# Loading Q and K weights in pieces of three, six and seven heads, and storing half-pass V rows in another row order, in a two-layer recurrent-attention and GLU kernel

## The chip, the cores and the metric

The kernel runs on one core of a Trainium2 chip. The metric is the device time of one execution in microseconds, given as a median of several runs; lower is better. The profile is one execution recorded by the hardware profiler, and its times are microseconds from the start of its span unless marked ns. PE is TensorE (PEld its weight loads), ACT ScalarE, DVE VectorE, POOL GpSimd and SP SyncE; SP and POOL issue the DMAs here.

## The reference

Two blocks alternate twice with the same weights: A, attention that carries a memory of 8 rows from one segment of 32 tokens to the next, and B, a gated feed-forward layer. All data are bfloat16.

```python
# x (1,2048,512), mem0 (1,8,512), Wq/Wk/Wv (512,32,128), Wo (32,128,512)
# w_gate/w_up (512,1792), w_down (1792,512)
def A(x, mem0, Wq, Wk, Wv, Wo):
    mem, outs = mem0, []
    for s in range(64):                                    # one segment after another
        h = concat([mem, x[:, 32*s:32*(s+1)]], axis=1)     # 8 + 32 rows
        q, k, v = (einsum('btd,dhe->bhte', h, W) for W in (Wq, Wk, Wv))
        p = softmax(where(mask, q @ k.T * 128**-0.5, -1e9))
        o = einsum('bhte,hed->btd', p @ v, Wo)
        mem = o[:, :8]                                     # goes to the next segment
        outs.append(o[:, 8:])
    return concat(outs, axis=1)
def B(x): return (sigmoid(x @ w_gate) * (x @ w_up)) @ w_down
x = x + A(layernorm(x)); x = x + B(layernorm(x))
x = x + A(layernorm(x)); x = x + B(layernorm(x))
```

The mask (`(idx[:, None] < 8) | (idx[:, None] >= idx[None, :])` over the 40 rows) is causal for the segment's rows and open for the memory rows; it is the same for all segments.

## The kernel before

**Steps.** The 64 segments of a layer must go one after another, because each gives the next its memory rows. The kernel runs 70 steps; step t works on segment t of the first layer and on segment t-6 of the second together, 80 columns of activations (40 where only one layer has a segment). The heads go in pairs u and 16+u, three pairs to a group: heads 0 to 2 with 16 to 18, then 3 to 5 with 19 to 21, and so on, the last group being heads 15 and 31. A group's work is Q and K projections (L890), scores (L904), softmax on DVE and ACT, the transposition of the probabilities (L947), their product with V (L973) and the output projection (L991). Feed-forward blocks of 128 rows (L1093, L1117) and layer norms with their transposes (L662, L1061) are woven into the steps.

**V at the start.** The V rows of x don't depend on the memory, so those of the first blocks of the first layer are computed ahead, in passes of 128 rows by 512 columns (`v_pass`, matmuls L693). A piece of 64 rows that is left over goes through `v_half` (L730): its two halves of columns lie in partitions 0 to 63 and 64 to 127 of a bank, and of each 64 rows 32 belong to one octet of rows of four segments and 32 to two octets of two segments, put there by `take_part`. V rows of 32 rows go as strips (L815). A pass is evacuated by ACT or DVE casts (L1230, L1232) into one of nine boot buffers; these are the tiles of the feed-forward weight rings (wd, wg and wu, three each), which have no other use yet. From there DMAs on SP or POOL (L1226) store the rows in a DRAM scratch, scr, of which each step later loads its own into vsb. A boot buffer may be filled again once its store has landed.

**Weight loads.** `load_weights` adds all of them as SP tasks (L592): Wv in eight pieces of four heads (512 KB), and for each group of heads Wq, Wk and Wo in a piece for the heads u and one for the heads 16+u. A piece of three heads of Wq or Wk has rows of 768 bytes in DRAM, four per partition; a piece of one head has rows of 256 bytes.

**Order.** Nothing is issued as the code is written. Each operation is a task of a planner, with engines that may do it, a duration, a latency, the bytes moved and the buffers that it needs. A list scheduler (`forward`) gives each free engine the ready task of highest rank, and the ranks of all tasks are a string in the source, SEQUENCE, that `plan` decodes:

```python
for k, (q,) in enumerate(struct.iter_unpack("<H", code)):
    T[left.pop(q)].tail = -float(k)
```

The planner's estimates of when a DMA lands come from `lat` and `nb`. From the planned times `warm` also decides where filler matmuls on a constant tile, `hot` (L1216), go: before a planned gap of more than 250 ns on PE, up to some hundreds of ns each. Engines run their own instruction lists in order. SP's DMAs use eight semaphores in turn, so each SP DMA waits until the one eight before it has landed, and a store on SP that waits for its cast holds up the loads behind it.

The diff moves lines a little: those up to L600 stand one line higher in the changed kernel, those from L620 on two lines lower.

Of the kernel before, what the change touches and what calls it, by code (L numbers as in the profile page):

```python
# [53 lines left out]
;Aht@pIrb8fB#p5?Q#$k*OKvZZTq^c3OM%bV44b=*R*ZTyW=(F)eXpo=!dnjd%&eFWe?4v9B9J-6{(d-LCut;#!E)o@XKL;|1Yh}DX~>av(XnTcNY5yDmuUNDYpk)1hbP~Icf*@B%SY3<$N!PMdC+w  # L54
TzC*H?wh$B-*Ih~y~Z^1eU45ybkQ1*)!rl+2M7#!1kA=M>_00gM+A4yerPR?|M?Mj6^>>JOVW=CEf+cd3@>&Nfi0vId6NWR);FU?#N7i-E<e}?kQ5;smk7+$yR>6M$&vA+ka>GT!8=_b4-#fP#)eF7
^yFAVNqaBx;!Z*DxPH}w4u4hwLD|Xk-(55Lk^B_BDfkRj%d!v=C<*w7SG;+fg+&T)>)vE^_U=fY&kC>YwKQIya^N!=lH>FlpJ`Jr&lF|=A)fY+g;i{E@r#X;(VDk3V2MMXacuh+Y1k_asM6Wlyelal
#hat)UmCRL92k7baU(yGZ`~C!81W~7P5Erk>AYc<Vay?}YFcMj2ofpnp$(sP&YA3~nf~n+b1fFy?|Zym`QSa144a*IfxPvGj&Q1ek!IqLN$jiF41N6_7PG1D?N__fhI#wYegIrLSdO>RI&L#ADzYcB
9Qqa8r^xHgLyr2s6(Q^~qr%E_$NJ+TpJ_bc{R>AcDm>XZ4K<5#ddGdVwMU;&cRuZ|Sp~k`OZ$e|X_~sQ@384vzE1LEOy7FI`;?xf^#@MMQ)L6bC_!Zn4S4CHx9Vjn^H}pFj3R+|IJ2mzre;noNVd$S
`{%;vED%u54cw3M^F8VWNicF9{B~XUq?7A1595()pJ)9U7U(TRXvIYfie-lrSI2C)aZ1BBh3$_bQ;!I-B=8ScYh1ck&O!bB=K^(6{|r6Qx~A%7Guq$r@Iax)(DGfYMGmfWTtN`TiNx0^a_h-)zaQ;Y
Bg~_fxFI1YgW5VrkU}+v(OG0q+i!<|tAlPcRfvDusTf+wG<zAh-6L;+Y1?sI#2|g1{X&hwViH*}otG=?Uzck!7(XzcfK!b2s0y$`SNOr$pn;5(vR*N@6t6GIu9c&BiE<wNN?P(QqaXRd3M2ScK!LD`  # L60
7NE8fpYJ@UG|VxPeYSAG0la_&djDUlCG|bBoZOzAT#$(zHi(qOLpXAuXb5%<ke>jX1k1`o2(mU?ngq;3!G;hMQLm2&9MTEUYd^USvXFM#vQ$cKmjg>LrQvGCuN0;hmD;jcN{gk}oA#{rr~t7er6x;>
4TAPsm6b5FLH-g|Nf9h4giYb{D&c`|4)4`L+JTg9TM;~}=IotkUY(*Y!dPX~EqzNqLnvA&8*(y?XY|Ec+`KUE@_SSE)gkFi<&UF6JtvvpbP{*<I0G^z6$#&pA}^v95^Q4FK#<`jp&L`QSey9`{hytp
ep4|DPRnnzJfR5<$bbinu=f`jwczBNxe3uhZ<*z*5#J~4a?5s>6axJof)V}FxLuSWLQ`X$p%|GAo3ni>PtV+JzEAC$o%TiCe#d7B$K5bY%WL%|Y?`a4x@DA(YsP8dw{qC8hys!6@G=TJ3;?U)VFlx0
p<M<>KJllT(z)CRu8?`e3^R_R7%q?S32qi7rh98c7=(LFh!0=aD^hH1fNfXqg+Sja7$z4P_WGLKlHYlxk!E{x!eD5T8C@MZ?8P+s8nOs}&1S4ol`b-NnC>Xi=go6~%Yjg-4mHO!zq-ODIoX(~$HahI
@>xN0b)~I`DIDj5VKMa;CZ!v*mkbmOJ)#~W9x(W_v;<nswK`+PTq}ipg*!qKSltnE+$xw7Xt>R@wAQgZ(cg;enc1@7fR_`9(15bKuOa8wjwP|W7E?oWno808^?XT*fvZ96JauH_vO6Tmg0YAX{%<GP
x&vaN_I%f%_>nw(eGPl2kX+vA>jgyX^`O19337j8ctxfD{|+Geiw9%@3fRrZv?20mB-ZcAf?E$T01iSEPFlGkD*OepKVV{in{2e29t=mMTqiEZTBE&ID`7X6Mk+WhT~yUj_1`*B0!BsL3UYqo?S%Vq
U~wE&tp6ZiVbg<Vu#-btWwj?J)D@CYb1QP&m*#PL94pnFvBWYRVkl3T5;SG{PpgL>Y&7Ql1a;Xg%4O>TI04XhhFijc@Xaj9&%wm+O^!e2Is7ho@U?|Mv)s#Z>S-JQQ#^hP6vJ~o=FQdi%0==QiO4>}
e22-8{8_Hk?+)?_0!^US$Hin*eL}LmU1~LxfMwEBA4T-2y4BQI`Q`64rb)aYczym_%e@Wk1AuUFK%C=ysBJZCRbO!Y(YYGT<zd6Mwt&h>Ca^n2NDBRxQWx&kPPPClqibM>xRMi&j62;fUA|z^Rcv5p
F-MNEhkhZ`GG5|d;IIVWX3i~0UVC9j1JR_k)g}?mU=2&5>*Rm+{_7pfxv?)^BxJ;D;a}CKd+}lN*i{g!Cy29Nm6fs_s@A?29$S^C=sV2}7Gf8_q&p!Q-YYz<B<R6Q_L7&#1<{@t2|<x!)7#Viogyj%
#-k9m4_)fkps3Y)zWP9b))iXN6jc_5mj%JnzCGR%<`NT61>o}26adbxHKRWL;eGC_dPO$_0O%g3i&ylcjeO4Kp62wN^0l#G6AFX@sZ^p&lw_s>8|c<!RV%n$fDjRZ^Xo3)dI6V@-wLB+#PD@hFC|K{  # L70
hmxDVz+rV(-EotTD{>}bC$E+{l9$s&EXe`8-@_@{(5~Q9mF~S=mCXo-n@iGREv|B+hO}uaWNVIcBn--!6`yjXIwzk;tw$!|KNqC$<@Mh~wq+c2tXd(#Sr5!A-C=djQjW|zR>pY8ZsJpuHW?k&Vb2JQ
uK|mZtO+LXNgAg_(QsnAn`7TMhXkU87ogepo>y~+Q6YK~1|}aZxCTk*_)GF*LQIhh36&7b>}*Sf3aF_c%*8+#IpW86KlVU=PpvHDgCV0ph`o{zROB--HMhg)Z{yqq7Md>tmspIb4I7+>36}snbBa~p
2aq{FMm-sS@IOYq2mBa3IjrPDLfH_wb!L?PC1T|kd4ugY$iW8dl9Wn@+q#mR|8AO(pY8)gqHT0JZH)K^N=vOt<7^u-*$(l~x1U$PlUtaJALTr+N%)sKo=X09?|my^)5C^3SE4k&!$P)9kk;k6_2g=+
Xo<ZissDeGX{x7oi<<eTlp~=irUE^K35dz<U*p)9mm+d=#S6VL#4*xk?AUu>i@32H9Xk7!kk_K%&o5%^Sg@sug$7E7OfE13qWWUI<gX~Ww=Ovk<b`gMnA(LF)GbK-eGV(1eZq-0q2A1%j71R50jC+4
(YzP{LgPu!joT@AK^rRGm+vVYvgOLUd8rkU;M*n6fXUc#<4{U(<*Jw%^s|AolsW{O5e?q{R_5NdEk8h+662I+)Aqfs4y9uUn};G(N@<LuFs|^cT2FPBk6;o7V$@9XgP@*E$knBwHr>Rl>{fn#3`Kt?
yh8LxMxizaxtE9ijw|3QBSBOL8_*nr`Ija$bn=z6WE8x*$~+<;`&N15!cf9T9fLAG-W%WU!ZwOoz+`YmAGo$BFvfAhCU$wVm+!7~hqUD?_Qj=5pJZxrj>B%sT+T>^Mpe?7D7;6#U{20sx38&r-oZv<
@f;0J3*rnK+>gY7iHrU98Tc!cU$yG52J(53IMpe}CyZMp-M}xnkjatQP^<S=pQKx;v4)WilNu5`<Za2;cEYv!A-^%SNfLQcZHw<TrO#PTqr1ut(uD2lWlxw84HtnVFYJyK21!>3Pf#x4_<auBIOT|n
+@;+PE;I~5c;iLu7VSwLd!<@@giENcHgyQSL;-J2%c`n1>tw)5Bs}veFA<rH!^3m=l`VY}Nszs5V--R@?57p?P(+>mj+CH3TAIxks-M;?YeONKMhQ_kw+?5>kTJHu|7yVyF>aFUs;2k$08rksLjZ&}
Rec5D4v+VLqz!LXr1aXx264-a^;D{bA9Zt}4bb>Bb_oPv)r^`d2*V&n2Ps(kqh|OKVk6^jP`eI67p;O+<c~o`+;F|9sQaL-_ZCgX_3J6psL~YuH;xzf`)FU$t#f-U$eq7GKrs6{7FHkpW}34-RKFM*
9&x(UP}Ft7D%r_qN6h*20^EO0T}Wm?E1yp5ENr4Ju^T6EzeEMp)Bxm$T|rJ-CxTow#WGfD?k-in)T%Z8GRC)%u=eaRl_Ei`LMbFvL;YDLA~vt~$m$JHk6jxGBe&YFI+>Nh?*OuRiCPnCt@Nm2(HxK7  # L80
#&3kRM`t_Q;5~4|e>TMT4t<3*yUdt-xWMmna~NN*hW^#KJ3(n?D%%4`{Q+jJuR0q4-_lBy1j+FBqmip{O6sP`{bVE4hNzX|>QS_7B!LY(zVBx%^%(gHKijzO7Ss7Y(G2Y2VQ+E`6%mA5j&X?^I+)=|
P<db;>vgq@xzey}P_~g3{N0R$zl8UO=BM~MHCS_OrtXQ46onh0Y#OYaL!ZE2hoY+*G}tq}KBV|{#L!ZpbzLAaT=ge(F?IDIVMCq|mJBTHQ7CK5JO9=<=;)u%Yj;dLVc$R@gieZ`3AQh;6$rQ@iQZ@=
V>RB0haCzv329qrPHxI7KHybS8kD}@tey_pdZ+S3^+1!Zd_u(#@Bwc51(75!RI^zH@e*z62rR(bpoRk@rSm4S)S>3R3(Wmz*PCj{K$|na6?y2wU-w!(O%p6C9;oB8ZWV&<g-`Z^=HY<$y{^Z}jzCH3
UV$HD&VAwr6NtQ=vm`Xi+b-%FeG1g-5T&0ujXOTbNIQ{--zb|ZXytJtlj%7Tc{m1gKrfa#1X|V|As@F`7PH^zsG86&KLMk?>yZwc_JoAGr4WCLyeG~q5GD-oSX}2SSUvbPtzotDQV0E)5@I+Lha>C&
DS}ZGSn^mAJ`rlJm$5wePawoBajMO_l>j@?a2^U6_XSpq6S=J&H%kq4yvh*XzCIoZEU5NZczw6pMsmG}ABT=!bK@{MoQf~)lh)A0R22|G2BZt657mYk*_Tox-<g_09hV%;nL)YWonN|3AoDDx&1bL#
na*q83IB<G*_XVk%zy^teDZs~klOgm%HrUN2`M2h$pxj`RxaLf?mzW9jL{u4b|2D$NCMsLEnv^EJh#UKVL&G@cccOKTX~vm=xXk>U(k{q><I@&qD4ep%cxk8wmbLK%on{EPuT3?KiL3BsfB_s1}bzk
4k|w0K9P#^uUS|!0xaU$hu;r;-r3W&(`9`69^o6k9MDHHCCOPN>8OGEB7kEu=OXx}z3lSM@#1-PR{12eGz$@r>xDR@OeAgi{t+wvo>a0$WAP0PR9xFiZje_>iXPbTL!I&>UXu+LdY@e1wZR>E17rZB
_+1n?x+n@BHD(xyH5M3>DojQSVA(+cjxuKoi`As`(3r341mYa=<Gnp#T0tV^_cl4vhHpPKWj~AM*68j?JL({AjU)?K8UBd2%9vf(4s6E?TZ5#2(31QOu_voI?SmO95M~gstN^S&ygMVMa+7$!j~~*w
>n0u^sTKie_itwQlu@d`$Zj>onhtI!b0vvzI)BHLoRI$U?9LZM)w3v7pp8=Wpl7T(#6V4<Yi}9FIZDO+1savChV`Bwh!a{l%y(g|5;5s7w^124BDWWQHs3LPqOE<c0yvy1C^1zPbcI>H>xn!)3D3@R
0ejF8VuC8mkDGEa&ISH)g{aX_*WmOWBZF4(w=N*V^Q|3g%A^g5GeDl>1C_i%H2H#=*lDDJa2^QLXVdUf&jgBJXyA@u?p3@x%H%c$e0#Fu<fvQcuJ;TBqCnx9iYc^$QG7^^dbn&AkGoUyANwJZSqPhK  # L90
Ac>4^b;;ty(xTHUj2Jk&pY&#O3PT@VMEmFVd&dixCF6K<_$liKg3Cj*V%4jhO3@Wv#1C|H^oLjrm!TiSpn57#u77vrsh{=&Bkb^MTE8UmD`d-2n0-lFoX^MDTotFvOL_g{o`^VVLKK*p6%^F6_vHwy
L%E;$n_9PyS)iahe;p1n{}jFulI{!Q1ducj@Bbp282b;W9E58@b2ydomxZm{=_sh)pl*hMxqO1J>PY^+m4UKxeO8+f+8jLgrYvd@;1y27j3(5TF_=J=u{nd(<XyYI*}vjdwexVPNW<`~(nxQV`Q3bm
?-oKCugIcU$CVRPsibT<&C{`K8rw`m={?5dMI#P67pVd5XXX!^kt#O7jdXHtpC<=aQ_M-IF1c$;XZ^`K2CoLbmqR$Ivq{#PQJlH<ka(UMG@!Wy?g!OE;NF9YA=d6(hACy`S2&ca19}PpzuBXTH08Tu
@Lz?f1zQpJ>%+nhM7NU7yh@DH3;cUaFfmvXqEpg)AVAQFNWD5-cvZBj8C+?m#N=#2Gz`(7O!lBeMK#0m|1R1c7XDoN+Wi~qW$PQ}4iTimXzlVCmsLkEz@waJu_xEIADt!`c|AG5*imf6#OId*7Omc%
qaSm5>$72OwOoYELPh^-&@7Cs=@8jZsTMRf!amf|sTUxf>V*{4CGsTvibsUK&XTPA+hHsZ3PI1D<FlDN+@A@t933*jJ1!OX*s2Pp$90mq4+}v0yg#t*hCdVr+krL5Y2j14j40Fk8#jZ7N*okytgprx
RoHXPQ>sp|qSDHq>3xvdg;+6VhrdRa&E_m8?%9AM0TPy1JQMu{){ovpB9COdT^_c<EN`3f$n$c_`mRbTrd}lj^xn?M>P}XdptxnwQf0TIqV&^G9k3bqu^`cP>6-h=l3S1LvjFU*kOXblPG4e&Z--0E
+KhA|kTn<6k|h`R`SZ$l@Oss%2G~13Q-M0VSk1Z`OA9`BGJ=fH_Oc3Xv<Fj}eMi@iZ>m!MW2RF5Y@NbA;&M@_i@z@lO}~Tk2qmy$XZgEXy*xS3zgC_1$wK@jWjKs|ETZb2|0cV;KeBM8Uew32FhHk<
g2?JK%8cPAmwQ$OY6r?+a;<v(-M7Hlwh@ahq}H<85-$X?@JSbXE2?g5?(sr-a(*h{<wT>lJ=Q#V6#SmiIfE3+i=WW-Uc3Bi+M*W2C~08AQAXzaep+y0(7sVh)!;#B2t36^j}s4`QIIT`gP<(b<y}U;
# [361 lines left out]
class Kern:  # L460
# [123 lines left out]
    def load_weights(self):  # L584
# [20 lines left out]
        for heads, us in self.groups:  # L605
            n = len(us)
            for nm, sb, v in (("wq", self.wq, wq_v), ("wk", self.wk, wk_v)):
                for h0 in heads[:2]:
                    cs = slice(h0 * P, (h0 + n) * P)
                    ld(sb[:, :, cs], v[:, :, cs], P * self.DC * n * P * 2, [(nm, h) for h in range(h0, h0 + n)])  # L610
# [685 lines left out]
```

## Time and profile before

| | us |
|---|---|
| median of seven runs | 1787.61 |
| the runs | 1785.46, 1788.23, 1787.61, 1787.39, 1784.75, 1788.11, 1788.02 |
| the profiled execution | 1790.12 |
| its span | 1788.4 |
| PE busy | 1768.1 (99% of the span) |
| DVE, ACT, POOL busy | 1142.9 (64%), 1166.7 (65%), 575.4 (32%) |
| DMA moved | 270.66 MB, 151 GB/s over the span |

The profiled execution takes 1.7 us more than its span, for what lies around it. "Busy" of an engine counts its instructions' time, waits excluded; the granted clock is the share of full speed that the throttle left to TensorE. The DMA share is the mean busy share of the core's 16 DMA engines; packets overlap a little, so that it can stand slightly above 1. A row of waits names the waiting engine and line, what released it, the total, how often and the longest.

### The profile page before, as it was taken

How to read it: one execution, taken by the hardware profiler on the slowest of the kernel's cores; microseconds unless marked ns; L12 is line 12 of the kernel's file. 1: busy time of each engine (PE TensorE's matmuls, PEld its weight loads, DVE VectorE, ACT ScalarE, POOL GpSimd, SP SyncE). 2: the span in 40 equal slices, each digit the busy share in tenths (PEclk: the TensorE clock that was granted, in tenths of full speed). 3: DMA queues.
4: the chain of work that ended last, by engine and by line, in shares of the span. 5: the costliest groups of instructions: out<-in, count | busy, mean ns of one | idle time of the engine just before them, and what ended most of it. 6: DMA issues, size and time to landing. Idle time of an engine off the chain costs nothing.

```text
span 1788.4 us, 92192 instructions
## 1 busy us (share of the span) xinstructions
PE 1768.1 (99%) x40077; PEld 1518.7 (85%) x40077; DVE 1142.9 (64%) x3944; ACT 1166.7 (65%) x2960; POOL 575.4 (32%) x827
## 2 busy tenths in 40 slices
PE   9899999999999999999999999999999999999998
PEld 4588888989898898889898898988888888988886
DVE  4367566766667567656666676657656765666665
ACT  5566656666666667666766666666666666666564
POOL 4313031413333242323324231333324232333332
PEclk9999999999999999999999999999999999999999
DMA  9824354635555464455546453555556454555543
GB/s 317 275 79 141 85 153 114 182 105 158 165 152 159 135 175 121 139 149 166 159 127 201 134 155 105 162 159 167 154 147 174 113 146 132 159 153 148 155 141 94
DMA packets 138599, 270.66 MB, mean 151 GB/s; under 512 B 32954, under 2 KB 71746, under 8 KB 138194
## 3 DMA queue, kind: packets, MB, share of 16 engines
q0 software_dynamic: 56624, 181.91, 34.6%
q1 hardware_dynamic: 81570, 82.86, 16.4%
q8 instruction: 314, 5.14, 1.2%
q14 instruction: 91, 0.75, 0.1%
HBM read 220.41 MB, written 25.69 MB: 138 GB/s over the span
## 4 chain that ended last, share of the span: by engine, by line
PE 93%; DVE 2%; DMA 2%; issue 1%; ACT 1%; POOL 1%; SPq 0%; ACTq 0%; DVEq 0%; POOLq 0%
PE bank L890 33%; PE bank L991 16%; PE bank L1093 11%; PE bank L815 7%; PE bank L693 7%; PE bank L1117 5%; PE bank L973 4%; PE bank L904 4%; PE bank L947 2%; PE bank L1216 1%; PE bank L662 1%; DVE st L918 1%; PE bank L1061 1%; DMA wo_sb<-in_A_Wo_dram 0%; DVE pb L935 0%
## 5 line engine op out<-in xcount | busy, mean ns | idle before, releaser
L890 PE MATMUL bank<-hT,wk_sb 128*128 128x80 bf16 (+1 forms) x8960 | 621.8, 198 | 0.7 <-issue 0.6
L890 PE MATMUL bank<-hT,wq_sb 128*128 128x80 bf16 (+1 forms) x8960 | 622.0, 198 | 0.0
L1230 ACT CAST qku<-bank 128x480 bf16<-128x480 f32 (+3 forms) x770 | 388.6, 513 | 220.8 <-PE bank L890 138.8
L890 PEld LDWEIGHTS <-wq_sb 128*128 128x128 bf16 x8960 | 454.4, 99 | 34.1 <-issue 23.1
L890 PEld LDWEIGHTS <-wk_sb 128*128 128x128 bf16 x8960 | 450.7, 99 | 1.0 <-issue 0.9
L918 DVE TENSOR_TENSOR st<-bank,cst 40x240 f32<-40x240 f32 (+3 forms) x768 | 278.4, 368 | 188.7 <-PE bank L904 180.9
L991 PE MATMUL bank<-otsb,wo_sb 128*128 128x80 bf16 (+1 forms) x8960 | 363.8, 198 | 2.2 <-DMA wo_sb<-in_A_Wo_dram 1.2
L991 PEld LDWEIGHTS <-wo_sb 128*128 128x128 bf16 x8960 | 336.9, 99 | 17.9 <-issue 2.0
L1230 ACT CAST otsb<-bank 128x480 bf16<-128x480 f32 (+3 forms) x420 | 199.8, 483 | 65.1 <-PE bank L973 52.1
L1086 POOL DMA_DIRECT2D wu<-in_B_w_up_dram x217 | 164.4, 758 | 240.3 <-PE bank L1093 96.3
L1085 POOL DMA_DIRECT2D wg<-in_B_w_gate_dram x217 | 164.4, 758 | 237.5 <-PE bank L1093 92.5
L1111 POOL DMA_DIRECT2D wd<-in_B_w_down_dram x217 | 154.2, 711 | 221.9 <-PE bank L904 75.6
L928 ACT ACTIVATE st<-st 80x240 f32<-80x240 f32 (+3 forms) x420 | 159.4, 381 | 37.1 <-DVE st L925 34.7
L652 POOL TENSOR_TENSOR small<-small,cst 128x1 f32<-128x1 f32 (+1 forms) x80 | 45.2, 567 | 427.8 <-DVE small L651 427.5
L1093 PE MATMUL bank<-xnT,wg 128*128 128x128 bf16 (+2 forms) x1784 | 171.7, 218 | 0.6 <-issue 0.5
L1093 PE MATMUL bank<-xnT,wu 128*128 128x128 bf16 (+2 forms) x1784 | 171.0, 218 | 0.0
L930 DVE TENSOR_REDUCE small<-st 80x6 f32<-80x240 f32 (+3 forms) x420 | 151.0, 361 | 19.6 <-ACT st L928 17.4
L904 PE MATMUL bank<-qku 128*128 128x80 bf16 (+1 forms) x2240 | 160.1, 198 | 1.0 <-DVE pb L935 0.5
L925 DVE TENSOR_TENSOR st<-st,small 80x240 f32<-80x240 f32 (+3 forms) x420 | 154.6, 369 | 3.1
L935 DVE TENSOR_TENSOR pb<-st,small 80x240 bf16<-80x240 f32 (+3 forms) x420 | 153.9, 369 | 4.0
L923 DVE TENSOR_REDUCE small<-st 80x6 f32<-80x240 f32 (+3 forms) x420 | 151.6, 362 | 4.1
L973 PE MATMUL bank<-ptsb,vsb 104*128 104x80 bf16 x2048 | 139.3, 199 | 1.2 <-ACT ptsb L1230 0.2
(103 smaller groups left out, 2384.1 us busy)
## 6 DMA issues: line engine op xcount, KB each, us to landing
wg<-in_B_w_gate_dram POOLq DMA_DIRECT2D x220, 256.0 KB, 4.3
wu<-in_B_w_up_dram POOLq DMA_DIRECT2D x220, 256.0 KB, 4.4
wd<-in_B_w_down_dram POOLq DMA_DIRECT2D x220, 256.0 KB, 4.4
vsb<-scr SPq DMA_DIRECT2D x460, 48.0 KB
vsb<-sst SPq DMA_DIRECT2D x464, 32.0 KB
scr<-vst SPq DMA_DIRECT2D x112, 96.0 KB
wv_sb<-in_A_Wv_dram SPq DMA_DIRECT2D x8, 512.0 KB
wq_sb<-in_A_Wq_dram SPq DMA_DIRECT2D x10, 384.0 KB
```

Source lines behind the costliest of these rows:

```text
L890: nc.tensor.matmul(o_ap, lhsT=W[:, c, h * P:(h + 1) * P], rhs=mv(c), start=(c == 0), stop=(c == DC - 1))
L904: nc.tensor.matmul(s_all(SB)[:, w0 + i, :], lhsT=fview(qku[:, i, 0, 0:1], [(1, P)]), rhs=qku[:, i, 1, 0:ncol], start=True, stop=True)
L918: pl.add("DVE", dve_ns(n, True), lambda gsz=gsz, hs=hs, st=st, SB=SB, pj_=pj_, npj_=npj_, mk=mk, idx=idx: nc.vector.tensor_tensor(out=st[p ...
L925: pl.add("DVE", dve_ns(n), lambda gsz=gsz, hs=hs, st=st, mx=mx: nc.vector.tensor_tensor(out=st[pr, hs], in0=st[pr, hs], in1=mx[pr, hs].uns ...
L928: pl.add("ACT", act_ns(n), lambda hs=hs, st=st: nc.scalar.activation(out=st[pr, hs], in_=st[pr, hs], func=ACTF.Exp, scale=self.scale), r=s ...
L973: nc.tensor.matmul(fview(OB[:, o:o + 1], [(ncol, 2), (1, L)]), lhsT=self.vsb[halves[u // 8]][0:64 + L, j, (u % 8) * P:(u % 8 + 1) * P], rh ...
L991: nc.tensor.matmul(WB[:, c * ncol:(c + 1) * ncol], lhsT=self.wo[:, h, c * P:(c + 1) * P], rhs=otsb[:, hl, 0:ncol], start=(h == 0 and c == ...
L1085: pl.add("POOL", 760, lambda wg=wg, fs=fs: nc.gpsimd.dma_start(out=wg[:], in_=self.wgv[:, :, fs]), r=[("wo", self.H - 1)], w=[gk] + bt, la ...
L1086: pl.add("POOL", 760, lambda wu=wu, fs=fs: nc.gpsimd.dma_start(out=wu[:], in_=self.wuv[:, :, fs]), r=[("wo", self.H - 1)], w=[uk] + bt, la ...
L1093: nc.tensor.matmul(gu[:, 2 * i + k, 0:n], lhsT=W[:, c, i * P:(i + 1) * P], rhs=xnT[:, c, rw], start=(c == 0), stop=(c == DC - 1))
L1111: pl.add("POOL", 760, lambda wd=wd, ip=ip: nc.gpsimd.dma_start(out=wd[:], in_=self.wdv[:, 2 * ip:2 * ip + 2, :]), w=[dk] + (["boot"] if se ...
L1230: nc.scalar.copy(out=dst, in_=src)
```

## The change

1. Wq and Wk are loaded in pieces of heads 0 to 2 and 16 to 18 (three heads, rows of 768 bytes), 3 to 8 and 19 to 24 (six heads, 1536 bytes), and 9 to 15 and 25 to 31 (seven heads, 1792 bytes): six DMAs per tensor in place of twelve. Wv and Wo are loaded as before.
2. Of a half-pass, the 32 rows of two segments by 16 rows lie in the buffer with the row, and not the segment, as the outer index (`take_part`), and the store to scr runs over them as 16 x 2 x 1024 elements in place of 2 x 16 x 1024 (`v_half`).
3. The planner's latency of a boot store goes from 4500 to 5000 ns, and its bytes for half-pass and strip stores from 65536 to 80000.
4. SEQUENCE is a new string, so the ranks of all tasks are new.

```diff
 SEQUENCE = r"""
-;Aht@pIrb8fB#p5?Q#$k*OKvZZTq^c3OM%bV44b=*R*ZTyW=(F)eXpo=!dnjd%&eFWe?4v9B9J-6{(d-LCut;#!E)o@XKL;|1Yh}DX~>av(XnTcNY5yDmuUNDYpk)1hbP~Icf*@B%SY3<$N!PMdC+w
...
+;Ag)rXk7pcfB%7A@!gH@5PER9zwFwU*Txh6(FIfkX|(7J?i&Gymhh!kX3<9*It9&+^ANuZ3nQF%vjb@k;)ADNDw~7A&yK6rftjYT<(0_Cu$F5_QL}_k&+#M$g4fMAuI3%VR%9II^4edG>hLecVFKKZ
...
+        parts = {0: 3, 3: 6, 9: 7}
         for heads, us in self.groups:
             n = len(us)
             for nm, sb, v in (("wq", self.wq, wq_v), ("wk", self.wk, wk_v)):
                 for h0 in heads[:2]:
-                    cs = slice(h0 * P, (h0 + n) * P)
-                    ld(sb[:, :, cs], v[:, :, cs], P * self.DC * n * P * 2, [(nm, h) for h in range(h0, h0 + n)])
+                    m = parts.get(us[0])
+                    if m:
+                        cs = slice(h0 * P, (h0 + m) * P)
+                        ld(sb[:, :, cs], v[:, :, cs], P * self.DC * m * P * 2, [(nm, h) for h in range(h0, h0 + m)])
...
-                       lambda vs=vs, d=d, c0=c0, n=n: ("dma", d, vs[c0:c0 + BLK * n, 0:512 * w]), lat=3000.0 + 1500.0 * boot,
+                       lambda vs=vs, d=d, c0=c0, n=n: ("dma", d, vs[c0:c0 + BLK * n, 0:512 * w]), lat=3000.0 + 2000.0 * boot,
...
-        dst = fview(tile[:, 0, c0:c0 + 1], [(P, self.DC), (n, 2), (1, n)])
+        dst = fview(tile[:, 0, c0:c0 + 1], [(P, self.DC), (1, 2), (2, n)])
...
-                                     (32, d.rearrange("(i r) e -> i r e", i=BLK)[i16:i16 + 2, r16:r16 + 16], (r16 // 8, r16 // 8 + 1))):
+                                     (32, d.rearrange("(i r) e -> r i e", i=BLK)[r16:r16 + 16, i16:i16 + 2], (r16 // 8, r16 // 8 + 1))):
                     pl.add(("SP", "POOL") if boot else "SP", {"SP": 650, "POOL": 650} if boot else 650,
-                           lambda lo=lo, i=i, dd=dd, flat=flat: ("dma", dd, flat()[64 * i + lo:64 * i + lo + 32, :]), lat=3000.0 + 1500.0 * boot,
-                           r=[(sb, 0), (sb, 1)] + (["boot"] if boot else []), use=[sb], nb=65536,
+                           lambda lo=lo, i=i, dd=dd, flat=flat: ("dma", dd, flat()[64 * i + lo:64 * i + lo + 32, :]), lat=3000.0 + 2000.0 * boot,
+                           r=[(sb, 0), (sb, 1)] + (["boot"] if boot else []), use=[sb], nb=80000,
...
-                        r=[(sb, 0), (sb, 1)], w=[("vd", j, b, q8, kk) for kk in (2 * i, 2 * i + 1)], lat=3000.0, use=[sb], nb=65536)
+                        r=[(sb, 0), (sb, 1)], w=[("vd", j, b, q8, kk) for kk in (2 * i, 2 * i + 1)], lat=3000.0, use=[sb], nb=80000)
```

## The prediction

> **What bounds the kernel now.** I read the page first. TensorE is busy 99% of the span in every slice; the DMA engines are full only in the first two slices (some 90 us) and near half afterwards.
>
> ```profile
> PE 1768.1 (99%) x40077; PEld 1518.7 (85%) x40077; DVE 1142.9 (64%) x3944; ACT 1166.7 (65%) x2960; POOL 575.4 (32%) x827
> ...
> PE   9899999999999999999999999999999999999998
> ...
> DMA  9824354635555464455546453555556454555543
> ```
>
> Then the windows by stage (window and its length, busy time of PE, PEld, DVE, ACT and POOL, granted clock, DMA share, GB/s):
>
> ```profile
> 15.00:30.00 15.00, 15.00 (x138) 7.92 (x136) 8.75 (x32) 8.97 (x19) 8.17 (x14) 1.00 1.04 321
> 45.00:60.00 15.00, 14.01 (x119) 7.28 (x117) 3.29 (x10) 7.43 (x15) 7.48 (x14) 1.00 0.92 283
> 60.00:75.00 15.00, 12.49 (x112) 5.71 (x112) 1.57 (x5) 9.20 (x18) 5.35 (x10) 0.89 0.97 307
> 75.00:90.00 15.00, 13.79 (x353) 10.67 (x350) 9.45 (x35) 10.15 (x30) 3.17 (x6) 1.00 0.71 228
> 600.00:900.00 300.00, 299.60 (x6771) 264.47 (x6768) 194.58 (x673) 202.15 (x503) 99.94 (x138) 1.00 0.53 153
> ```
>
> From 300 to 1500 us TensorE works 298.3 to 299.6 of every 300 us: nothing to win there. What a load or store can still move lies between 45 and 90 us, where the DMA share is 0.7 to 1.0 and PE loses a few us. The waits of PE name them (total, times, longest), and the timeline gives their places; the line at 21.82 is an undisturbed group of the same 16 matmuls:
>
> ```profile
> PE bank L693 <- ACT wu L1230: 3.5, 1, 3.5
> PE bank L991 <- DMA wo_sb<-in_A_Wo_dram: 1.2, 1, 1.2
> ```
> ```profile
> 21.82 3.63 PE L693 MATMUL bank<-wv_sb,xvf 128*128 128x512 bf16 x16
> ...
> 62.51 5.30 PE L693 MATMUL bank<-wv_sb,xvf 128*128 128x512 bf16 x16 [3.51 <-ACT wu L1230]
> ...
> 87.75 0.97 PE L991 MATMUL bank<-otsb,wo_sb 128*128 128x40 bf16 x32 [1.22 <-DMA wo_sb<-in_A_Wo_dram]
> ```
>
> After the 3.51 us stop the same work takes 5.30 instead of 3.63 us, and the windows show why: the granted clock is 0.68 and then 0.80.
>
> ```profile
> 62.50:66.00 3.50, 3.49 (x12) 1.38 (x12) 0.00 (x0) 3.39 (x7) 2.17 (x4) 0.68 1.06 338
> 66.00:69.00 3.00, 3.00 (x30) 1.17 (x32) 0.00 (x0) 1.33 (x3) 0.22 (x1) 0.80 1.06 360
> ```
>
> The chain of waits tells who was late (start, duration, what):
>
> ```profile
> 54.79 1.57 SPq L592
> ...
> 56.46 5.32 DMA scr<-wu
> ...
> 61.88 0.59 ACT wu L1230
> ```
>
> A boot V pass could not be evacuated because the buffer wu was still being stored, and that store was issued only at 56.46, behind a three-head K load on SP (L592), and took 5.3 us while the DMA engines stood at 1.03 to 1.09. The wo wait at 87.75 is the same kind: those loads were queued on SP behind a store that waited until 78.3 for ACT.
>
> **The change, part by part.**
>
> (1) Q and K loads. Before, each tensor comes in ten 3-head pieces (768 B rows) and two 1-head pieces (256 B rows), after in two pieces each of 3, 6 and 7 heads (768, 1536, 1792 B): 24 DMAs become 12. Bytes stay. The packet records of the first 95 us give the median on one engine: 256 B 18 ns, 768 B 36, 1024 B 46, 2048 B 84 (means 19, 38, 51, 99). Before: 10240 packets of 768 B take 24.6 us of all 16 engines and 2048 of 256 B 2.4 us (sums of the records): 27.0. After: 2048 packets each of 768 (38 ns), 1536 and 1792 B; between 1024 and 2048 I read off 66 and 76 ns: 2048x(38+66+76)/16 = 23.0 us. So 4.0 us of DMA time less, out of some 84.5 us in the first 95. The Trainium skill, "DMA: Bandwidth & Descriptors", section Specifications, speaks against this: it puts the line rate at transfers of 512 B and more, so 768 B rows would already be as good as longer ones and only the 256 B rows would improve, to a third of the time of a 768 B packet each: 2.4 minus 2048x12/16 = 1.5, 0.9 us. The rows here still climb from 21 B/ns at 768 through 22 to 24 at 2048, so I take 4.0 and keep 0.9 as the low end; by the rule the queue would stay 3.1 us longer, and the sum would be that of rival A below, 1785.5. None of this is span by itself: PE waits for no Q or K load. It only shortens the queue in which stores and wo loads stand.
>
> (2) The order. The whole schedule is a new list; this is where time can move. The DMA work queued by the time PE has done 22.9 us of its work rises from 40.0 to 45.7 us (SP and POOL together), since 45 instead of 28 of the 64 Q/K head loads are ahead of that point. In return the SP stores that follow (V rows whose matmuls end at PE positions 31.8 to 37.5, some 46 to 52 us) no longer have a big load between them; before, wq, a store, wk and the late wu store alternated there with SP issue times of 2.36, 2.19 and 1.57 us. The last three wo loads stand ahead of the store that waits for PE position 62, with their need at 65.1 to 67.5. Walking through both queues with the packet times, I find no boot buffer whose store lands after it is wanted and no late wo piece. Gains: -3.51 (stop), -1.67 (5.30 less 3.63, slow clock after it), -1.22 (wo). Bounds for each: nothing, if the wait only moves, to the whole.
>
> POOL's queue gets one DMA more (833 for 832 instructions of its own) and SP 13 fewer (1364 for 1377), 12 of them these loads. SP issues in order and each of its DMAs waits for the one eight before it, so behind a 7-head piece (2.43 us of DMA) that is not through stands everything later on SP: the wv pieces (last needed at PE position 17.3; I find some 2 us in hand) and the V stores. That is the slower rival below.
>
> (3) Fillers. The kernel puts warming matmuls (L1216, 0.213 us each at full clock) before planned gaps. Before first transposes 38.25 units become 43.0, up to the first V pass 8.5 become 6.25, and 1.75 are new before the first QK: +4.25 x 0.213 = +0.9 us; PE is not waiting for anything there in the trace (fillers run up to the transposes), so I take it as real. At 75 to 150 us 2.75 fewer: at most -0.6, and nothing where they only filled a wait; I take -0.4. At the end 5.0 become 8.0: +0.6 at most, 0 if they cover waits (gaps in the last 89 us are 3.1 us, fills 2.6); I take +0.6.
>
> (4) Half-pass stores with 16 rows outermost instead of 2. Four boot stores of 64 KB, and four later ones. The other rule to weigh is in the same page, section "Why a DMA increments its semaphore by 16 and not by 1": the slowest dimension sets over how many engines a DMA is spread, so 2x16 would use two engines and 16x2 all sixteen. By rule: 32 packets of 84 ns are 1.34 us on two engines, 0.17 on sixteen, some 1.2 us sooner for each of four stores. By row: the four boot 2x16 stores on POOL landed 6.7, 6.2, 5.75 and 6.2 us after issue, beside 6.1, 5.8 and 5.8 of their neighbours with eight rows outermost: 0.2 us apart. I take 0 on the path; by the rule one such store on the path would give 1.2 us more, 1782.3 in place of 1783.5. The take_part copy has the same elements in another order: 0, two ACT or DVE copies per half pass with both engines at 65%; if the stride costs, it is under the 0.3 us of such a copy and hidden beside V matmuls.
>
> (5) The planner's longer store latency costs nothing itself; it shifts orders. In the steady part, the places that must be tight are equally many in both orders (oxT transposes right behind the last Wo matmul 8 times, next QK within 223 ns of PE work 4 times), so 0, within 1 us each way.
>
> Sum: -3.51 - 1.67 - 1.22 + 0.9 - 0.4 + 0.6 = -5.3 us on the profiled execution of 1790.12 (span 1788.4): 1784.8. The profiled one is 2.5 us above the median 1787.61, and the seven runs fall in two at 1785 and five at 1788. If the stall is in the plain runs as in the profiled one, they go to 1782.3; if the 2.5 us are part of the stall and absent there, to 1784.8. I take the middle, 1783.5.
>
> **Rivals.** A difference under 0.2% (3.6 us: 1784.0 to 1791.2) is about what a measurement of this kernel cannot tell from no change.
>
> Rival A, the wait moves on. The DMA share is 0.9 to 1.07 all the way to 75 us before, and 4 of 84 us less does not empty it; a store that lands in time here makes the next one the last. For: POOL's stores landed 2.2 to 7.5 us after issue (median 5.7), so the 5.3 us of the late one was no exception. Against: only one buffer was short in 95 us. Half of the 6.4 us stays, with the fillers: -3.2 +1.1 = -2.1, 1785.5; nearly all of it stays: 1788.
>
> Rival B, slower: the front-loaded six- and seven-head pieces. Place: 30 to 55 us, SP's queue. 5.7 us more DMA work stands ahead of the V stores and the last wv pieces. If those land later by more than the slack, a boot buffer comes free late at one more place, each at the price of the old one, 3.5 + 1.7 us. Old stall kept (the wo wait too), one new, fillers +1.1: 1787.61 + 5.2 + 1.1 = 1793.9; a new one in place of the old, with the wo wait gone: 1787.61 + 1.1 - 1.2 = 1787.5. It decides once the new waits exceed the old by 2.5 us, that is once two boot buffers, or one by twice as much, come free too late: a store that lands some 8 us after issue instead of 5.3, twice. For: DMA is full there. Against: the stores are spread over POOL's queue too, and the queue is drained by 46 us in my walk.
>
> Rival C, the edit doesn't do what it says: rows gain nothing (0.9 us) and half-pass stores were as fast; then only the order counts, and the number is the forecast's or rival A's.
>
> **Chances.** Forecast with everything going (1782.3 to 1784.8): 0.43, of which 0.33 under 1784.0 and 0.10 above; more than that (store latencies fall with the emptier queue, or the steady part gains 1 us): 0.15, faster; rival A (and C's part of it): 0.25, all within 0.2%; rival B: 0.17, about 0.15 over 1791.2 and 0.02 within. Faster 0.48, same 0.37, slower 0.15. The range runs from 1780.5 (forecast less the steady part's 1 us and a little DMA gain) to 1790.5 (rival A and the mild end of B); what is left out is B's bulk and a little below. For the faster cases alone it would be 1780.5 to 1784.
>
> **What would show it.** Right: in PE's waits no L693 wait for an ACT cast over 0.5 us, no wo wait at L991, granted clock 1.00 in all windows from 15 to 110 us; the window 45 to 90 us with 44 us or more of PE busy (40.3 now); first V pass at 14.9 instead of 14.24; packets of 1536 B near 66 ns and of 1792 B near 76. Wrong: a wait of over 2 us at an L693 or L815 evacuation with a store named before it, or wv named as releaser; the clock under 1.0 behind it; PE gaps at 300 to 1500 us above 6 us in all.

## The result, and the profile after

The changed kernel takes 1782.9 us (median of 11 runs, 1781.49 to 1785.24) against 1788.11 us before (29 runs, 1784.75 to 1790.82): a ratio of 0.9972 with a 95% interval of 0.9964 to 0.9979, 5.2 us faster. The profiled executions stand 6.9 us apart (1783.2 and 1790.12, spans 1781.4 and 1788.4). The forecast was 1783.5.

The page after; the busy rows are as before, and PE has no thin slice at the start (the second of the 40 stood at 8 of 10 before):

```profile
PE 1765.0 (99%) x40083; PEld 1517.2 (85%) x40083; DVE 1144.3 (64%) x3931; ACT 1167.6 (66%) x2973; POOL 573.8 (32%) x828
...
PE   9999999999999999999999999999999999999998
...
DMA  9825254635555464445546453555555454555543
```

The windows after, same columns. Between 45 and 90 us PE now works 44.98 of 45 us (before 40.28), the clock is 1.00 throughout, and DMA's work is over sooner (0.51 from 75 to 90 us, before 0.71). The steady part is unchanged.

```profile
15.00:30.00 15.00, 14.98 (x139) 7.80 (x137) 6.38 (x23) 10.63 (x26) 8.55 (x16) 1.00 1.06 344
45.00:60.00 15.00, 14.98 (x124) 7.73 (x123) 3.99 (x11) 9.42 (x18) 8.08 (x15) 1.00 0.90 290
60.00:75.00 15.00, 15.00 (x237) 8.78 (x236) 5.36 (x16) 10.13 (x21) 4.12 (x8) 1.00 0.97 324
75.00:90.00 15.00, 15.00 (x410) 11.71 (x409) 8.32 (x33) 10.10 (x29) 3.38 (x7) 1.00 0.51 163
600.00:900.00 300.00, 299.51 (x6761) 263.74 (x6759) 195.57 (x671) 199.77 (x496) 99.99 (x139) 1.00 0.53 152
```

Of PE's waits (total, times, longest) both boot rows are gone; what stands at the top are the oxT transposes that were there before. New are a wait of 1.1 us for a vsb load and most of the 2.3 us at L892 for which the profile names no releaser (0.6 us before):

```profile
PE bank L1063 <- ACT oxT L1232: 3.5, 8, 0.5
PE bank L892 <- issue: 2.3, 2, 1.1
PE bank L975 <- DMA vsb<-sst: 1.1, 1, 1.1
PE bank L1218 <- DVE small L564: 1.0, 1, 1.0
```

The timeline at the two places: V matmuls run through (24 in 5.54 us, full pace) and the last Wo group has no bracket with an idle time before it.

```profile
57.80 5.54 PE L695 MATMUL bank<-wv_sb,xvf 128*128 128x512 bf16 x24
...
81.89 0.96 PE L993 MATMUL bank<-otsb,wo_sb 128*128 128x40 bf16 x32
```

To see where the 7 us of the profiled span were won, I weighted every matmul of PE other than fillers with the median start-to-start time of its kind in the trace before, and compared the times at which the two traces had done equal work (after minus before):

| PE work done, us | 15 | 45 | 50 | 65 | 70 | 100 | 200 | 500 | 1400 | end |
|---|---|---|---|---|---|---|---|---|---|---|
| difference, us | 0.0 | +0.7 | -4.5 | -4.5 | -5.9 | -6.5 | -5.7 | -4.6 | -5.0 | -7.2 |

The steps: +0.7 over the start, -5.2 at the old stop, -1.4 at the old Wo wait, then 1.9 us up and 2.6 us down to the end.

### The profile page after: what moved, and what is told of

It reads as the page before. It is cut to its first block, busy times and chain, and to the rows that moved or that the text cites. A ratio compares the mean times of both kernels' runs of the same rounds, so it can differ in the third digit from the quotient of the medians.

```text
span 1781.4 us, 92187 instructions
## 1 busy us (share of the span) xinstructions
PE 1765.0 (99%) x40083; PEld 1517.2 (85%) x40083; DVE 1144.3 (64%) x3931; ACT 1167.6 (66%) x2973; POOL 573.8 (32%) x828
## 4 chain that ended last, share of the span: by engine, by line
PE 96%; DVE 2%; ACT 1%; issue 0%; SPq 0%; DMA 0%; POOL 0%; ACTq 0%; DVEq 0%; POOLq 0%
PE bank L892 33%; PE bank L993 17%; PE bank L1095 11%; PE bank L695 8%; PE bank L817 8%; PE bank L1119 5%; PE bank L906 4%; PE bank L975 4%; PE bank L949 2%; PE bank L1218 1%; PE bank L664 1%; DVE st L920 1%; PE bank L1063 1%; DVE small L932 0%; DVE small L925 0%
## 5 line engine op out<-in xcount | busy, mean ns | idle before, releaser
L892 PE MATMUL bank<-hT,wk_sb 128*128 128x80 bf16 (+1 forms) x8960 | 622.4, 198 | 1.2 <-issue 1.1
L892 PE MATMUL bank<-hT,wq_sb 128*128 128x80 bf16 (+1 forms) x8960 | 622.4, 198 | 1.2 <-issue 1.1
L892 PEld LDWEIGHTS <-wq_sb 128*128 128x128 bf16 x8960 | 454.1, 99 | 35.5 <-issue 25.6
L892 PEld LDWEIGHTS <-wk_sb 128*128 128x128 bf16 x8960 | 450.8, 99 | 1.5 <-issue 1.4
```

The costliest lines, as they stand in the source:

```text
L892: nc.tensor.matmul(o_ap, lhsT=W[:, c, h * P:(h + 1) * P], rhs=mv(c), start=(c == 0), stop=(c == DC - 1))
```

## The experiments

Times are medians, ratios are to the kernel before on the same chip (1787.14 us for the first four, 1788.07 us for the others). One execution of each kernel is profiled, and it can stand anywhere in the scatter of its runs.

**The old order with four SP tasks moved.**

```diff
         order = self.pl.plan()
+        sp = [tk for tk in order if tk.on == "SP"]
+        for a, b, late in ((55, 65, 1), (54, 65, 1), (52, 65, 1), (80, 84, 1)):   # a goes behind b in SP's queue
+            order.remove(sp[a - 1])
+            order.insert(order.index(sp[b - 1]) + late, sp[a - 1])
```

> The kernel before with its narrow loads and its own order, except that four SP tasks are moved: the K load of heads 12 to 14, the K load of head 31 and the Q load of heads 28 to 30 go from ahead of the late wu store to behind the K load of heads 3 to 5, and the wd store that waits for ACT until 78.3 us goes behind the wo loads of heads 25 to 27, 31, 12 to 14 and 15. Position theory (the stalls are places in SP's queue): both waits go or nearly so, the L693 wait falls from 3.5 us to under 1 us, the clock behind it is 1.00, no wo wait; 1788.1 - 5 = some 1783. Row theory (the 3 us of DMA time that wider rows save is what made the store land in time): the store still lands late because the same DMA work is outstanding, 2 us or more of wait stay with a slowed clock, 1786 or more.

Measured: 1788.12 us, ratio 1.0003 (0.9994 to 1.0012): no gain. Its waits, and the window with the Wo waits:

```profile
PE bank L991 <- DMA wo_sb<-in_A_Wo_dram: 1.8, 2, 1.5
PE bank L693 <- ACT wu L1234: 1.2, 1, 1.2
...
PE bank L890 <- DMA wk_sb<-in_A_Wk_dram: 1.0, 1, 1.0
```
```profile
75.00:90.00 15.00, 13.07 (x281) 9.38 (x280) 6.38 (x26) 8.42 (x25) 3.76 (x7) 0.89 0.74 237
```

The late store came sooner, the wait for it fell from 3.5 to 1.2 us and the clock stayed at 1.00 there; but a K load is now late by 1.0 us and the Wo loads by 1.8, although the store that stood ahead of them now stands behind. The slow clock moved with the wait: it was 1.00 from 75 to 90 us before, and is 0.89 here, with 0.50 from 86.6 to 90.0 us behind a Wo wait of 1.5 us. At equal work against the trace before, 4.0 us are won at the old stop, 1.1 lost again at the K load and 2.3 about the Wo wait, some 1.7 of them by the slow clock. This is rival A, the wait that moves on. That both boot waits were the fault of two misplaced tasks falls with it: in the old order the loads behind them land at their deadlines too.

**The load edit alone, in the old order.** The first task of a set in SP's order loads the whole set, the others issue nothing.

```diff
-                    cs = slice(h0 * P, (h0 + n) * P)
-                    ld(sb[:, :, cs], v[:, :, cs], P * self.DC * n * P * 2, [(nm, h) for h in range(h0, h0 + n)])
+                    g0, m = {0: (0, 3), 1: (3, 6), 2: (3, 6), 3: (9, 7), 4: (9, 7), 5: (9, 7)}[us[0] // 3]
+                    cs = slice((h0 - us[0] + g0) * P, (h0 - us[0] + g0 + m) * P)
+                    k = (nm, h0 - us[0] + g0)
+                    self.first_of(sb, v, cs, k, P * self.DC * n * P * 2, [(nm, h) for h in range(h0, h0 + n)])
...
```

> The kernel before with its own order, but the first task of each set of heads 3 to 8, 9 to 15, 19 to 24 and 25 to 31 loads the whole set in one DMA with rows of 1536 or 1792 bytes, and the other tasks of the set issue nothing. So the load edit alone, in the old order. Row theory and position theory both take most of the stall away here: ahead of the late wu store 3 us of DMA work are gone or earlier, and SP issues three loads fewer there: L693 wait under 1.5 us. They differ in the second wait: the wd store still stands ahead of four wo loads on SP, so by the position theory the wo wait of 1.2 us stays (1788.1 - 4.5 = 1783.6), by the row theory it shrinks with the DMA load to under 0.5 us (1782.5). If the front-loaded wide pieces hurt the early V stores or the wv pieces (the slower rival), a new wait appears between 25 and 55 us and the time is 1788 or above.

Measured: 1792.04 us, ratio 1.0027 (1.0018 to 1.0035), slower than before. The V stop is gone, but two waits for loads stand in its place, of a kind that neither theory expected; the chain of waits gives the second load's issue and the time to its landing:

```profile
PE bank L902 <- DMA wq_sb<-in_A_Wq_dram: 3.5, 1, 3.5
PE bank L902 <- DMA wk_sb<-in_A_Wk_dram: 3.1, 1, 3.1
```
```profile
41.22 14.32 DMA wk_sb<-in_A_Wk_dram
```
```profile
45.00:60.00 15.00, 8.40 (x76) 4.53 (x75) 2.20 (x7) 4.66 (x10) 5.93 (x12) 0.77 0.87 324
```

The wide pieces moved more, 20.3 MB by 60 us in place of 18.6 (sums of the packet records), but the wrong bytes: heads 12 to 15 and 28 to 31, which the old order needs only at PE positions from 58 on, came with heads 9 to 11 and 25 to 27, which it needs from position 35 on (48.7 us in this trace). The two late loads are Q and K of heads 25 to 31: the only packets of 1792 B after 39 us run from 43 to 55 us, and PE went on at 52.1 and 55.6 us. A larger piece takes the deadline of its first head, and in this order it landed late. The trace doesn't account for the whole of the slower median: the profiled execution is the fastest of the eleven (1788.65 us, the profiled one before took 1790.12), and at the end of its work it stands 1.7 us ahead of the trace before. What the slower executions lose beyond this is not shown.

**The new order with narrower rows.** Three kernels keep the changed kernel's order and split each load of six or seven heads into several DMAs within its task (the cut shows the three variants one below the other):

```diff
-                        cs = slice(h0 * P, (h0 + m) * P)
-                        ld(sb[:, :, cs], v[:, :, cs], P * self.DC * m * P * 2, [(nm, h) for h in range(h0, h0 + m)])
+                        # by heads, 768 and 1024 B rows:
+                        cut = [(slice(0, 4), slice(h0 * P, (h0 + 3) * P)), (slice(0, 4), slice((h0 + 3) * P, (h0 + m) * P))][:1 + (m > 3)]
+                        # or by chunks, 1536 and 1792 B rows:
+                        cut = [(slice(c, c + (4 if m == 3 else 2)), slice(h0 * P, (h0 + m) * P)) for c in (0, 2)][:1 + (m > 3)]
+                        # or as before, 768 and 256 B rows:
+                        cut = [(slice(0, 4), slice((h0 + i) * P, (h0 + min(i + 3, m)) * P)) for i in range(0, m, 3)]
...
+                            for c, cs in cut:
+                                nc.sync.dma_start(out=sb[:, c, cs], in_=v[:, c, cs])
```

> The changed kernel with its order, but each load of six or seven heads is issued as two DMAs by heads (3 and 3, 3 and 4), rows of 768 and 1024 bytes. From the packet medians (36, 46, 65, 74 ns) the eight loads take 2048 x (36+36+36+46)/16 = 19.7 us in place of 2048 x (65+74)/16 = 17.8 us, 1.9 us more of DMA time, and eight DMAs more on SP's eight semaphores. Position theory: within 1 us of the changed kernel and of the same loads split without narrowing rows, 1783 to 1784. Row theory: about two thirds of the 3 us saved are given back, a stall of 2 us or more returns, 1785 to 1787.

> The changed kernel with its order, but each load of six or seven heads is issued as two DMAs by two of the four 128-row chunks each, rows still 1536 and 1792 bytes: the same number of DMAs as in the split by heads, at the wide rows. Both theories: as the changed kernel, 1783 within 1 us, unless the eight more DMAs on SP (each some 0.4 us to issue, and one more turn of the eight semaphores) make a store late; then both splits lose the same.

> The changed kernel with its order, but every load of six heads is issued as two DMAs of three heads and every load of seven as three of 3, 3 and 1 heads: the row sizes and the number of Q and K DMAs of the kernel before (10240 packets of 768 B, 2048 of 256 B, 24 DMAs) in the new order. DMA time of these loads 27 us in place of 24. Order theory (what matters is which load or store stands where, and the new order has DMA time to spare): no wait at L695 or at Wo, 1783 to 1784. Row theory (the new order stands only with the 3 us saved): bytes moved by 60 us fall from 19.8 to under 19 MB, and waits of 2 us or more in all come back between 50 and 90 us, 1785.5 or more.

Measured: by heads 1783.34 us (0.9976, 0.9965 to 0.9986), by chunks 1783.07 (0.9979, 0.9969 to 0.9988), with the rows and the number of loads of before 1783.33 (0.9971, 0.9962 to 0.9980). All three are the changed kernel within the intervals; none has a wait at a V pass or for a Q, K or Wo load. The last one settles the row theory: 24 DMAs of 768 and 256 B rows, 27.2 us of DMA time for Q and K against 27.0 before and 23.9 in the changed kernel, and the whole gain is there. What its windows show is where the room came from; before, these two had a DMA share of 0.92 and 0.97:

```profile
45.00:60.00 15.00, 14.98 (x124) 7.71 (x123) 4.12 (x11) 9.20 (x18) 7.93 (x15) 1.00 1.00 320
60.00:75.00 15.00, 15.00 (x238) 8.81 (x236) 5.23 (x15) 10.13 (x21) 4.13 (x9) 1.00 1.00 319
```

With the same packets it had moved 19.7 MB by 60 us (18.6 before; the row theory wanted under 19) and 24.5 MB by 75 us (23.2 before). The new order keeps the DMA engines supplied; the wider rows give 3 us of DMA time on top, and the changed kernel leaves them partly idle (0.90 in the first of these windows).

**A large load ahead of the V stores, in the new order.**

```diff
         order = self.pl.plan()
+        sp = [tk for tk in order if tk.on == "SP"]
+        for a, b, late in ((52, 46, 0), (53, 46, 0), (54, 46, 0)):   # a goes ahead of b in SP's queue
+            order.remove(sp[a - 1])
+            order.insert(order.index(sp[b - 1]) + late, sp[a - 1])
```

> The changed kernel, but the three six-head loads (Q of heads 19 to 24, K of 19 to 24, K of 3 to 8, 6.3 us of DMA time) are moved on SP from behind the stores of wd, wu, wu and wd at 47 to 53 us to ahead of them. Position theory (a boot store behind large loads lands late and stops a V pass): the old stall returns, 2 to 5 us at L695 with a store as the releaser and a granted clock under 0.9 after it, 1786 to 1790. If the number of bytes and not the place counts: no wait over 1 us, 1783 within 1 us.

Measured: 1784.90 us, ratio 0.9981 (0.9972 to 0.9990), some 2 us over the changed kernel; the profiled execution is 4.1 us over it (1787.33). The old stop is back as it was: chain of waits, timeline and windows say

```profile
53.26 8.33 DMA scr<-wu
61.69 0.59 ACT wu L1236
```
```profile
62.33 5.30 PE L695 MATMUL bank<-wv_sb,xvf 128*128 128x512 bf16 x16 [2.47 <-ACT wu L1236]
```
```profile
62.00:66.00 4.00, 3.67 (x10) 1.35 (x10) 0.00 (x0) 3.35 (x8) 2.20 (x4) 0.57 0.60 191
66.00:69.00 3.00, 3.00 (x36) 1.31 (x38) 0.00 (x0) 1.96 (x4) 0.46 (x1) 1.00 0.18 56
```

The store of 192 KB landed 8.3 us after its issue behind 6.3 us of loads, the pass behind it waited 2.5 us, and 16 matmuls took 5.30 us as before. By 60 us this kernel had moved more than any other, 21.0 MB: not the bytes but their order decides. This is the stop of rival B, provoked; in the median it costs less than the 1786 expected.

**The half-pass stores undone in the changed kernel.**

```diff
-        dst = fview(tile[:, 0, c0:c0 + 1], [(P, self.DC), (1, 2), (2, n)])
+        dst = fview(tile[:, 0, c0:c0 + 1], [(P, self.DC), (n, 2), (1, n)])
...
-                                     (32, d.rearrange("(i r) e -> r i e", i=BLK)[r16:r16 + 16, i16:i16 + 2], (r16 // 8, r16 // 8 + 1))):
+                                     (32, d.rearrange("(i r) e -> i r e", i=BLK)[i16:i16 + 2, r16:r16 + 16], (r16 // 8, r16 // 8 + 1))):
```

> The changed kernel with its order and loads, but take_part's layout and the half-pass stores as before (2 segments outermost, 2 x 16 x 1024). Theory that this edit is worth nothing: 1783 within 0.8 us, the four POOL stores of half passes land within 1 us of the same ones in the changed kernel. Theory that a store with 2 outermost uses two DMA engines and is slow: it lands over 1 us later, and since boot buffers are short there, a wait of 1 us or more appears at a boot V pass, 1784.5 or more.

Measured: 1784.19 us, ratio 0.9977 (0.9967 to 0.9988). The interval overlaps most of that of the changed kernel, and its boot stage has no wait at a V pass, as the first theory has it. The stores themselves speak for the second. By the trace the two on POOL landed 6.8 and 6.6 us after issue, against 5.1 and 5.7 us in the changed kernel, and the two on SP (all four were expected on POOL) 6.0 and 12.3 us, against 7.1 and 10.6: three are 1.0 to 1.7 us later, one is 1.1 us sooner. Each of the two on SP raises its semaphore in 3 steps in place of 16, which fits two engines better than sixteen. PE just doesn't wait for them. The 1.3 us between the medians, of 8 and 11 runs taken at different times, can be nothing or some 1 us; this is left open. In its profile 1.07 us of the distance lie in the fillers at the start (last section), where the edit has no part.

**Fewer fillers at the start.**

```diff
             fill = self.pl.warm(order)
+            k0 = max(list(fill)[:2], key=lambda i: fill[i][1])
+            fill[k0] = (fill[k0][0], fill[k0][1] - 28)
```

> The changed kernel with seven fewer filler matmuls (1.5 us at 0.213 us each) ahead of the first transposes, whose input xn is there at 10.5 us while the fillers run to 12.2. If the start is bound by the fillers and the DMA queue has room: everything starts 1.5 us earlier, 1781.4. If the DMA engines, full until 75 us, bound the stage: the 1.5 us come back as a wait on a load or store between 14 and 75 us, 1783.

Measured: 1782.65 us, 6 runs, ratio 0.9968 (0.9957 to 0.9980): not to be told from the changed kernel. In the trace the first real work starts 1.2 us earlier than there, and not the 1.5 us of seven fillers, since two more of the others were slow (10 for 8, last section). At equal work of 90 us and at the end 0.7 us are left of it. No wait of PE for a load or a boot buffer came up in the first 110 us, so no such wait takes the rest.

## Why the prediction was right

**The stop and the clock, -3.51 and -1.67.** Right in size: the step at that place is -5.2 us in the comparison of equal work. The reason given, a store behind large loads on SP with its landing stretched by a full queue, is shown by putting three loads ahead of it in the new order, which brings the stop and the slow clock back. It was incomplete: taking loads away from in front of it in the old order only passed the wait, and the slow clock, on to a K load and to Wo. The cure is the order of loads and of the work that needs them together; which of the new order's many moves matters most was not separated. One candidate was not tried: moving the boot stores that block SP while they wait for their casts to POOL. The record speaks against it as the whole reason: up to 95 us SP waits 7.0, 3.4 and 1.0 us for ACT's casts to wd, wg and wu before, and no less, 5.3, 3.9 and 3.0 us, in the changed kernel.

**The Wo wait, -1.22.** Right, -1.4.

**Step 1, the rows, was right in time and wrong in part.** I had 23.0 us for the loads after and 4.0 us less; the records give 23.9 and 3.1. The packets of 1536 and 1792 B took 65 and 74 ns in the median where 66 and 76 were read off; the step mixed medians for the long packets with means for the rest, and under load the means are 69 and 77. The rule of the Trainium skill in "DMA: Bandwidth & Descriptors", Specifications, that 512 B are enough, doesn't hold to this accuracy here (21 B/ns at 768, 24 at 1792), but the 1785.5 that the prediction hung on the rule didn't come either: with the old rows, and so with none of the 3.1 us, the new order takes the same 1783.3. The statement that the loads only shorten a queue was right, and that queue had room.

**Step 2, the walk through the queues,** found no late store and no late wo piece, and there is none. It had not seen how much room the new order has: 3 us of additional DMA time cost nothing.

**Step 3, the fillers.** At the start +0.7 came out where +0.9 stood; the changed kernel's trace had three slow fillers fewer, 0.6 us, by chance (last section), so the edit's own part is nearer +1.3. For the fillers at 75 to 150 us -0.4 stood, and -0.6 came out between the Wo wait and 100 us of work. At the end +0.6 was wrong: the added fillers lie for the most part in gaps that are idle otherwise (after 1500 us the fillers take 5.7 us for 5.2 before, and PE's listed waits 2.3 for 3.0), and 2.2 us are won after 1400 us of work, in pieces whose causes I can't assign. Against it stand 1.5 us lost from 100 to 1400 us, among them new waits of 1.2 and 0.9 us that end at 159 and 174 us and one of 1.1 us that ends at 571 us; the steady part was put at 0 within 1 us. The two misses, -2.8 and +1.5 us, cancel in part, which is luck.

**Step 4, the half-pass stores:** 0 was put down; the measurement allows 0 to about 1 us. The rule of the two engines was set aside too soon: with the stores undone, three of the four land 1.0 to 1.7 us later, near the 1.2 us that the prediction worked out by the rule. With four stores in a full queue this is a hint and no proof. PE waits for none of them, so nothing of it is seen on the path.

**From the profiled to the plain runs.** The forecast took the middle of 1782.3 (the stop is in the plain runs as profiled) and 1784.8 (it isn't wholly). 1782.9 lies between. For the profiled execution the sum said 1784.8, and 1783.2 came, 1.6 us less; that the median was hit within 0.6 us rests on the middle, for which there was no measurement, and is luck to that extent. The experiment with the stop provoked shows the same shape: 4.1 us in the profiled execution, 2.0 in the median. Why a stop and its slow clock are worth less in the median than in the profile is not shown, as no other execution was profiled.

**The rivals.** A didn't come in the changed kernel, but is what moving four tasks in the old order gives. B didn't come; its place and price are real (2.47 us and 1.67 us in the profile when provoked), and the load edit without the new order is slower by 0.27%, with waits beside B in its trace: Q and K pieces that are late themselves. C was right for the row sizes taken alone: they have no measurable share.

## What to carry to other kernels

Where weights stream in beside the first work, list for each load and store when it is needed and in which place of its queue it stands; bytes moved by a given time say nothing on their own (21.0 MB by 60 us gave a stop, 19.7 MB gave none). Merging loads moves the deadline of a whole piece to its first user, so merge only together with a new order of the work, and test the merge alone in the old order too. A single wait taken out of a full queue went to the next in line here: look at the DMA share around it before expecting its length as a gain.

## What the runs showed of the hardware

The clock at the start of the program rises after a number of slow matmuls that changes from one execution to the next. The fillers follow each other at 0.43 us at first and at 0.216 from some point on; in ten traces that point lay between 4.36 and 6.52 us, after 8 to 13 slow ones. So the same 43 fillers took 11.15 us in the changed kernel (8 slow) and 12.22 us in the one with the half-pass stores undone (13 slow):

```profile
1.00 11.15 PE L1218 MATMUL bank<-hot 128*128 128x512 bf16 x43 [1.00 <-DVE small L564]
```
```profile
1.00 12.22 PE L1218 MATMUL bank<-hot 128*128 128x512 bf16 x43 [1.00 <-DVE small L564]
```

At 0.21 us for each slow filler this is about 1 us of the scatter between runs, in a place where most of these edits don't act; a single trace of this kernel can't settle a difference of that size.

The slow clock after a stop costs the same after stops of different length: 16 matmuls took 5.30 us after a stop of 3.51 us and 5.30 us after one of 2.47 us, but 3.61 us, full pace, after 1.16 us. The traces' clock records show why: the clock stood at 0.50 for 3.41 us in each (from 63.78 us before, from 62.44 with the stop provoked), and half of 3.41 us is the 1.7 us that the matmuls lost. With the load edit alone, after waits of 3.5 and 3.1 us, it was 6.83 us, twice that. The length of one stop isn't the whole condition: no slow stretch followed the 1.22 us Wo wait before, but one of 3.41 us followed the Wo wait of 1.48 us in the old order with four tasks moved, 1.5 us after PE had gone on. The runs here don't show where the line lies.
